# A two-level Winograd down-projection: the fourth right form gets its own room, the fifth product moves to the left buffer, three buffers are dealt anew and two weight sums are made earlier

## The chip, the cores and the metric

The kernel runs on one core of one Trainium2 chip. The metric is device time in microseconds of one execution. Work is split over TensorE (PE, with its weight loads shown as PEld), VectorE (DVE), ScalarE (ACT), GpSimd (POOL) and SyncE (SP). SP, ACT and POOL also issue DMA transfers, each on a queue of its own, and an engine works through its instructions in the order in which they were written.

## The reference, cut to what matters

2048 tokens of width 1024 go through two branches, which are mixed with a gate per token:

```python
g = sigmoid((x * gate_w).sum(-1, keepdims=True))
a = A_ref(x, wqkv, wo)          # 32 heads of 32; each token attends to 8 keys, 2 apart; then @ wo
b = B_ref(x, w_gate, w_up, w_down)   # h = gelu(x @ w_gate) * (x @ w_up), 3584 wide; then h @ w_down
return g * a + (1 - g) * b
```

Since both branches end in a matrix product, the kernel makes them one: the left side is `(1 - g) * h` beside `g * o` (o is the attention's output before `wo`), the right side `w_down` above `wo`. Everything that the change touches, but for two weight sums near the start, belongs to this last product, here called the down-projection.

## The kernel before, in words

**Memory.** Almost all of SBUF is one tile, `arena`, and the kernel deals out its addresses by hand. In the down-projection it holds ten buffers of 18 KB a partition, `bufs[0]` to `bufs[9]`, each 18 K-tiles by 512 columns in bf16. `plan` (L893) says for each half of the tokens (`s` = 0 and 1) which name lives in which buffer. All 8 PSUM banks are one tile, `banks`.

**Order of work.** The first 500 us are units of matmuls for the query, key, value, gate and up projections (L366), with a planner (`bg`, `due`, `run_bg`) that lays background tasks for DVE between them: each task has a priority and a unit from which it may run, and `due` finishes it before a given unit. `sums_qk` (L456) is such a task. Its two parts make the sums of the query and key weights that units 2 to 17 need, in eight DVE instructions (L463). From about 510 us on the order is written out by hand in `down(s)` (L1065), called for s = 0 and then for s = 1.

**The down-projection.** For each half of the tokens the left matrix is cut in four (`A11` to `A22`), the right in four (`R11` to `R22`), and Winograd's seven products take the place of eight. They need sums of the left quarters (`S`, `S2`, `AD`, on DVE at L925) and of the right quarters (`T1` to `T4`, made early and kept in HBM as `t_d`). Some of these seven products are made by plain matmuls (`mm`, L1074). The others go through `level2` (L1038), which applies Winograd's scheme once more: four in `down(0)` (on T1, T2, T3, T4 in this order) and six in `down(1)` (R11, T1, T2, T3, T4, R22), ten in all.

**One second-level product.** `forms_L` (L1000) makes four sums of quarters of the left operand in a buffer of their own, `forms_R` (L1008) four of the right operand. Of these four instructions the first, second and fourth fill three quarters of a right form buffer, and the third writes over a quarter of the right operand itself, `q(0, 1)`. Then `level2` runs seven products, each of two column blocks (j = 0, 1) of nine 128x256 matmuls (L1047):

```python
prod(0, 0, lq(0, 0), rq(0, 0), ...)   prod(0, 0, lq(0, 1), rq(1, 0))
prod(1, 0, lf[:, 0], rf[:, 0], lambda j: cp(p5d[:, j, :], c(1, 0, j)))
prod(1, 1, lf[:, 1], rf[:, 1], ...)   prod(1, 1, lf[:, 2], rq(0, 1), ...)
prod(0, 1, lf[:, 3], rq(1, 1))        prod(1, 0, lq(1, 1), rf[:, 2])
```

All accumulate in four banks, each used in two halves of 256 columns (`c(i, h, j)`). Between products ACT copies partial results from half to half (`cp`, L1052). The third product's state is kept aside in SBUF as fp32, two blocks of 128x256 (`part5`), and DVE adds it at the end (`join`, L1032). Before the change `part5` lies in the fourth quarter of the right form buffer, which no form uses.

**The forms are kept for the second half.** In `down(0)` `store_F` (L990) writes the forms of T1, T3 and T4 to HBM from ACT's queue in the middle of their `level2`: 576 KB for the form that lies in the T buffer, back into its quarter of `t_d` (L991), and 1728 KB for the three others, to `r_d` (L992). In `down(1)` SP loads T with `load_T` (L842) and the three forms with `load_F` (L988). SP issues its loads in the written order, and each load waits until its buffer has been read for the last time, and until the transfer that stood eight places ahead among those of SP and ACT has landed.

**Buffers that matter.** In `down(0)`: T1 and the right forms R6 share buffer 1, so `forms_R(R6)` may begin only when T1 has been read for the last time; T3 and S are in buffer 8; L5 and L7 in 4, R5 and R7 in 5; T4 in 9 and R4 in 7. In `down(1)` buffer 9 holds A21, buffer 1 R21 and buffer 7 A22, all loaded near the end of `down(0)`.

Of the kernel before, what the change touches and what calls it, by code (L numbers as in the profile page):

```python
# [9 lines left out]
ALU = mybir.AluOpType  # L10
# [58 lines left out]
def kernel(  # L69
# [55 lines left out]
    h_d = [[tc.dram_tile([P, 4, k, SC], BF16, name=f"h_d{s}{e}") for e, k in enumerate((NE_, NPAIR - NE_))] for s in range(2)]  # L125
    o_d = [[tc.dram_tile([P, NT, SC], BF16, name=f"o_d{s}{c}") for c in range(2)] for s in range(2)]
    t_d = [tc.dram_tile([P, NK, SC], BF16, name=f"t_d{k}") for k in range(4)]
    r_d = {k: tc.dram_tile([P, 3 * (NK // 2) * (SC // 2)], BF16, name=f"r_d{k}") for k in (1, 3, 4)}
    w_c = {k: tc.dram_tile([P, NK, SC], BF16, name=f"w_c{k[0]}{k[1]}") for k in ((0, 0), (1, 0), (1, 1))}
    z_d = tc.dram_tile([HK, S], F32, name="z_d")  # L130
    g_d = tc.dram_tile([2, S], BF16, name="g_d")
# [5 lines left out]
    with tc.manual_schedule(engines={mybir.EngineType.PE, mybir.EngineType.DVE, mybir.EngineType.Activation,  # L137
# [55 lines left out]
        def flat(a):  # L193
            return a.rearrange("p a b -> p (a b)")
# [261 lines left out]
        def sums_qk(part):  # L456
            L11, L12, L21, L22 = wq
            S1, S2, S4 = sq
            for o_, a, b_, op in (((S1, L21, L22, ALU.add), (S2, S1, L11, ALU.subtract)),
                                  ((L21, L11, L21, ALU.subtract), (S4, L12, S2, ALU.subtract)))[part]:  # L460
                for hk in range(0, HK, 2):
                    g = lambda t_: flat(t_[:, hk:hk + 2, :])
                    TT(out=g(o_), in0=g(a), in1=g(b_), op=op)  # L463
                    yield 1.14
# [21 lines left out]
        def at_end(n, fn):  # L486
            post.setdefault(n, []).append(fn)

        def due(n, t):
            at(n, t.finish)  # L490
# [296 lines left out]
            x_form3(1)  # L787
            yield 2.4

        due(Q0, bg(sums_qk(0), 1, 1))  # L790
        due(Q0 + 1, bg(sums_qk(1), 1, 2))
        due(Q0 + NT, bg(late_forms(), 3, Q0 + 1))
        bg(gate_task(0), 0, 0)
# [90 lines left out]
        def tf_close():  # L884
            while tf_q[0] < N1:
# [6 lines left out]

        plan = [dict(A11=4, R11=5, A12=2, R21=7, A21=6, A22=3, T1=1, T2=9, S=8, AD=0, L5=4, R5=5, L6=7, R6=1,  # L893
                     T3=8, L7=4, R7=5, T4=9, L4=1, R4=7, R22=6),
                dict(A11=0, R11=4, L1=5, R1=8, A12=3, A21=9, R21=1, A22=7, T1=2, AD=6, S=0, T2=8, L5=4, R5=5, L6=1, R6=2,
                     T3=0, L7=4, R7=5, T4=8, L4=2, R4=1, R22=9, L3=4, R3=5)]
        u2 = regf(R_U2, 4 * SC).rearrange("p (j n) -> p j n", j=4)
        qs = regf(R_QS, 4 * SC).rearrange("p (j n) -> p j n", j=4)
# [83 lines left out]
                    load_T(B[k], int(k[1]))  # L982

        KH, HN = NK // 2, SC // 2
        NF = 3 * KH * HN

        def load_F(rf, k):
            nc.sync.dma_start(out=flat(rf)[:, 0:NF], in_=r_d[k][:])  # L988

        def store_F(rf, b, k):  # L990
            nc.scalar.dma_start(out=t_d[k - 1][:, 0:KH, HN:SC], in_=quarter(b, 0, 1))  # L991
            nc.scalar.dma_start(out=r_d[k][:], in_=flat(rf)[:, 0:NF])  # L992

        def quarter(b, kh, h):
            return b[:, kh * KH:(kh + 1) * KH, h * HN:(h + 1) * HN]
# [12 lines left out]
        def forms_R(f, b):  # L1008
            f = quads(f)
            q = lambda kh, h: quarter(b, kh, h)  # L1010
            for o_, a, b_, op in ((f[:, 0], q(0, 1), q(0, 0), ALU.subtract), (f[:, 1], q(1, 1), f[:, 0], ALU.subtract),
                                  (q(0, 1), q(1, 1), q(0, 1), ALU.subtract), (f[:, 2], q(1, 0), f[:, 1], ALU.subtract)):
                TT(out=o_, in0=a, in1=b_, op=op)  # L1013
                yield 1.3

# [9 lines left out]
                nc.scalar.activation(out=two_banks(bk, i, 0), in_=omgrep[:, SUP:SUP + SC].rearrange("p (a b) -> p a b", a=2),  # L1025
                                     func=ACT.Copy, scale=0.0)

        def part5(rf):
            return flat(rf)[:, 3 * KH * HN:3 * KH * HN + 4 * HN].bitcast(F32).rearrange("p (j n) -> p j n", j=2)

        def join(bk, rf, i):
            TT(out=two_banks(bk, i, 1), in0=two_banks(bk, i, 1), in1=part5(rf), op=ALU.add)  # L1032

        def joins(bk, rf):
            for i in range(2):
                join(bk, rf, i)

        def level2(bk, L, R, lf, rf, mid=None, mid2=None):  # L1038
            p5d = part5(rf)
            lf, rf = quads(lf), quads(rf)  # L1040
            lq, rq = lambda r, c: quarter(L, c, r), lambda r, c: quarter(R, r, c)
            c = lambda i, h, j: banks[:, bk[2 * i + j], h * HN:(h + 1) * HN]

            def prod(i, h, l, r, then=None):
                for j in range(2):
                    for kt in range(KH):
                        nc.tensor.matmul(c(i, h, j), lhsT=l[:, kt, j * P:(j + 1) * P], rhs=r[:, kt, :], start=False,  # L1047
                                         stop=(kt == KH - 1), skip_group_check=True)
# [12 lines left out]
            if mid2:  # L1061
                mid2()
            prod(1, 0, lq(1, 1), rf[:, 2])

        def down(s):  # L1065
# [23 lines left out]
            if last:  # L1089
                run(scale_task(A12, s, 0, 0, NE_))  # L1090
                level2(XT, A11, B["R11"], B["L1"], B["R1"])
                rest = pieces(scale_task(A21, s, 1, 0, NE_), comb_task(AD, A11, A21, ALU.subtract))
                take(rest, 1)
                joins(XT, B["R1"])
                for j in range(4):
                    nc.scalar.copy(out=u2[:, j, :], in_=XP[j])
                run(rest)
                load_F(B["R5"], 1)
                loads(s, "T2")
            else:  # L1100
                for j in range(4):
                    mm(XP[j], A11, B["R11"], j, True, 0, NK - 2)
                    if j == 0:
                        yield
                for j in range(4):
                    mm(XP[j], A11, B["R11"], j, True, NK - 2, NK)
# [47 lines left out]
            level2(VT, AD, B["T3"], B["L7"], B["R7"],  # L1154
                   lambda: (zero_left(XT), last or store_F(B["R7"], B["T3"], 3)))
            fl, fr = forms_L(B["L4"], A22), forms_R(B["R4"], B["T4"])
            if last:
                fr = ()
# [8 lines left out]
            run(fr)  # L1167
            for j in range(4):
                if j % 2 == 0:
                    join(VT, B["R7"], j // 2)  # L1170
# [4 lines left out]
            level2(XT, A22, B["T4"], B["L4"], B["R4"],  # L1175
                   lambda: zero_left(VT) if last else store_F(B["R4"], B["T4"], 4))
            joins(XT, B["R4"])
            if not last:
                N = Bs(1)
                rest = pieces(scale_task(N["A11"], 1, 0, 0, NE_), woven(forms_L(N["L1"], N["A11"]), forms_R(N["R1"], N["R11"])))  # L1180
# [4 lines left out]
                loads(1, "A12", "A21", "R21", "A22")  # L1185
                zero_left(XT)
            if last:
                R3 = B["R3"]
                level2(VT, A12, B["R22"], B["L3"], R3, lambda: join(VT, R3, 1),
                       lambda: (join(VT, R3, 0), [add_out(VP[j], qs[:, j, :], 0, 1, j) for j in range(2)]))  # L1190
# [89 lines left out]
```

## Time and profile before

| | |
|---|---|
| time, median of 3 runs (lowest to highest) | 722.19 us (721.89 to 722.2) |
| the profiled execution: its time; its span | 722.87 us; 721.1 us |
| granted TensorE clock, mean | 1.000 |
| PE busy, of the span | 708.0 us, 98% |
| DVE busy | 672.9 us, 93% |
| ACT, POOL busy | 328.9 us (46%), 134.5 us (19%) |
| L1047, 1260 matmuls of 128x256 | 138.9 us busy |
| L1074, 282 matmuls of 128x512 in `down` | 62.7 us busy |
| `forms_L` L1005 (40) and `forms_R` L1013 (28), one instruction | 1354 and 1355 ns |
| ACT copy L1052 to SBUF, one | 373 ns |
| DMA busy share, 545.6 to 559.5 us; 602.1 to 647.5 us | 0.23; 1.02 to 1.03 |

The span runs from the first to the last instruction; the execution's time has 1.8 us more around it. A matmul's record is longer than its share of the engine (273 ns for one of 128x256, while 1260 of them keep PE busy for 138.9 us, so one follows the other after 0.11 us), because they are pipelined. Times within the span are counted from its start. In a timeline row the number in brackets is how long the engine had been idle and what ended that; "issue" there means that the profile names nothing.

### The profile page before, as it was taken

What the parts mean: (1) busy time and instruction counts of PE and PEld (TensorE: products, weight loads), DVE (VectorE), ACT (ScalarE), POOL (GpSimd) and SP (SyncE); (2) the same over time, 40 slices, a digit from 0 to 9 for tenths busy, and PEclk for the clock granted to TensorE, in tenths of its full rate; (3) what the DMA queues carried; (4) which work ended last, traced back from release to release, by engine and by line L of the source; (5) the groups of instructions that cost most, each with busy time, mean ns of one, the idle gap of its engine ahead of it and who ended that gap; (6) DMA issues with size and microseconds to landing.
All of it is one profiled execution on the core that took longest, in us unless ns stands there. A gap on an engine that the chain in (4) does not pass through costs nothing. (4 is left out here: it accounts for less than half of the span.)

```text
span 721.1 us, 10757 instructions
## 1 busy us (share of the span) xinstructions
PE 708.0 (98%) x4051; PEld 408.2 (57%) x4107; DVE 672.9 (93%) x721; ACT 328.9 (46%) x600; POOL 134.5 (19%) x233
## 2 busy tenths in 40 slices
PE   8999999999999999999999999999999999999997
PEld 4466656655544444444444444444447886748886
DVE  3699989999999999999998999999989999899997
ACT  4554446444457665555555555555322321132421
POOL 1333444133201331222210000000210002110011
PEclk9999999999999999999999999999999999999999
DMA  9976644279273758573943846371891899995941
GB/s 275 283 179 223 225 141 142 93 245 312 96 212 125 240 188 253 171 236 128 282 146 120 278 143 213 108 285 60 326 415 48 323 351 389 413 428 212 365 162 60
DMA packets 95252, 160.27 MB, mean 222 GB/s; under 512 B 19312, under 2 KB 71824, under 8 KB 90848
## 3 DMA queue, kind: packets, MB, share of 16 engines
q1 hardware_dynamic: 74992, 103.69, 42.1%
q0 software_dynamic: 15984, 48.29, 19.0%
q10 hardware_dynamic: 4224, 7.60, 3.0%
q8 instruction: 32, 0.52, 0.3%
q14 instruction: 20, 0.16, 0.1%
HBM read 110.40 MB, written 54.14 MB: 228 GB/s over the span
## 5 line engine op out<-in xcount | busy, mean ns | idle before, releaser
L366 PE MATMUL banks<-arena 128*128 128x512 bf16 x2136 | 472.5, 379 | 4.8 <-DVE arena L403 1.4
L366 PEld LDWEIGHTS <-arena 128*128 128x128 bf16 x2184 | 240.4, 111 | 236.4 <-issue 8.4
L1047 PE MATMUL banks<-arena 128*128 128x256 bf16 x1260 | 138.9, 273 | 1.3 <-DVE arena L1013 1.2
L1047 PEld LDWEIGHTS <-arena 128*128 128x128 bf16 x1260 | 123.0, 98 | 17.3 <-DVE arena L1013 1.5
L403 DVE TENSOR_TENSOR arena<-banks,arena 128x1024 bf16<-128x1024 f32 x78 | 95.2, 1221 | 12.4 <-PE banks L366 7.2
L389 ACT COPY arena<-banks 128x512 f32<-128x512 f32 x78 | 45.8, 587 | 130.7 <-PE banks L366 130.7
L374 ACT CAST arena<-banks 128x512 bf16<-128x512 f32 x102 | 59.8, 586 | 42.6 <-PE banks L366 42.3
L745 DVE TENSOR_TENSOR arena<-arena 128x2048 bf16<-128x2048 bf16 x64 | 77.0, 1220 | 0.5
L752 DVE TENSOR_TENSOR arena<-arena 128x2048 bf16<-128x2048 bf16 (+2 forms) x96 | 73.9, 776 | 1.0
L598 DVE TENSOR_TENSOR arena<-arena 128x2048 bf16<-128x2048 bf16 x64 | 74.7, 1219 | 0.1
L1074 PE MATMUL banks<-arena 128*128 128x512 bf16 x282 | 62.7, 379 | 0.7 <-DMA arena<-w_c 0.4
L260 POOL DMA_DIRECT2D h_d<-arena x28 | 20.4, 730 | 227.3 <-DVE arena L254 196.5
L396 ACT COPY banks<-banks 128x512 f32<-128x512 f32 x78 | 44.5, 570 | 22.5 <-PE banks L366 19.4
L1005 DVE TENSOR_TENSOR arena<-arena 128x2304 bf16<-128x2304 bf16 x40 | 53.3, 1354 | 0.5
L384 ACT COPY banks<-banks 128x512 f32<-128x512 f32 x78 | 45.0, 576 | 13.5 <-PE banks L366 12.1
L1052 ACT COPY banks<-banks 128x256 f32<-128x256 f32 x60 | 21.4, 356 | 61.5 <-PE banks L1047 61.3
L1074 PEld LDWEIGHTS <-arena 128*128 128x128 bf16 x288 | 28.1, 98 | 34.2 <-issue 0.7
L925 DVE TENSOR_TENSOR arena<-arena 128x2048 bf16<-128x2048 bf16 (+1 forms) x40 | 41.8, 1112 | 2.0 <-DMA arena<-h_d 2.0
L323 DVE TENSOR_TENSOR arena<-arena 128x1024 bf16<-128x1024 bf16 x60 | 38.7, 686 | 2.3 <-DMA arena<-in_B_w_up_dram 1.8
L1013 DVE TENSOR_TENSOR arena<-arena 128x2304 bf16<-128x2304 bf16 x28 | 37.8, 1355 | 2.0 <-issue 1.8
L372 ACT ACTIVATE arena<-banks 128x512 bf16<-128x512 f32 x54 | 32.3, 597 | 15.5 <-PE banks L366 15.5
L254 DVE TENSOR_TENSOR arena<-arena 128x2048 bf16<-128x2048 bf16 x28 | 34.1, 1216 | 1.9 <-ACT arena L251 1.4
(90 smaller groups left out, 436.1 us busy)
## 6 DMA issues: line engine op xcount, KB each, us to landing
arena<-t_d SPq DMA_DIRECT2D x8, 2304.0 KB, 15.8
h_d<-arena POOLq DMA_DIRECT2D x28, 512.0 KB, 4.3
arena<-w_c SPq DMA_DIRECT2D x12, 1152.0 KB, 13.1
t_d<-arena POOLq DMA_DIRECT2D x36, 256.0 KB, 4.4
arena<-h_d SPq DMA_DIRECT2D x6, 1536.0 KB, 9.1
arena<-in_B_w_gate_dram SPq DMA_DIRECT2D x15, 512.0 KB, 5.8
arena<-in_B_w_up_dram SPq DMA_DIRECT2D x15, 512.0 KB, 4.7
arena<-in_B_w_down_dram SPq DMA_DIRECT2D x28, 256.0 KB, 6.9
```

What stands on the lines that cost most here:

```text
L366: self.pe = nc.tensor.matmul(ps, lhsT=self.L[form](kt), rhs=rhs[:, kt, :], start=(start and kt == 0), stop=(kt == HK - 1), skip_group_chec ...
L374: nc.scalar.copy(out=o_, in_=i_)
L384: nc.scalar.copy(out=self.Y, in_=self.X)
L389: nc.scalar.copy(out=self.p5s, in_=self.V)
L396: nc.scalar.copy(out=self.Z, in_=self.Y)
L403: TT(out=self.T[:, :, c2s], in0=pair, in1=self.p5s.rearrange("p (o n) -> p o n", o=1).to_broadcast([P, 2, SC]), op=ALU.add)
L598: TT(out=dst, in0=q.rearrange("p (o s) -> p o s", o=1).to_broadcast([P, NWIN, AC]), in1=_win_ap(k, [[-DIL, NWIN], [1, AC]]), op=ALU.mult)
L745: TT(out=prod2[(t // 2) % 2][:, t % 2], in0=ab, in1=_win_ap(v[:, t, HALO:HALO + AC], [[SJ, NJ], [-DIL, NWIN], [1, SJ]]), op=ALU.mult)
L752: TT(out=out_, in0=h(0), in1=h(1), op=ALU.add)
L1005: TT(out=o_, in0=a, in1=b_, op=op)
L1047: nc.tensor.matmul(c(i, h, j), lhsT=l[:, kt, j * P:(j + 1) * P], rhs=r[:, kt, :], start=False, stop=(kt == KH - 1), skip_group_check=True)
L1074: nc.tensor.matmul(ps, lhsT=L[:, i, j * P:(j + 1) * P], rhs=R[:, i, :], start=(start and q == 0), stop=(q == NK - 1), skip_group_check=not ...
```

## The change

It has four parts.

1. `forms_R` writes its third instruction's result, the form from `q(1, 1) - q(0, 1)`, into the fourth quarter of the right form buffer and no longer over the T operand. `level2` reads it there. `store_F` becomes one transfer of the whole buffer (2304 KB) and no longer writes to `t_d`; `load_F` loads the whole buffer, and `r_d` grows to fit.
2. `part5` moves to the left form buffer, over the first left form. As that form is still read by the second column block, both `cp` calls now stand behind the whole product.
3. In `plan` for s = 1, R11 moves from buffer 4 to 8, L1 from 5 to 4 and R1 from 8 to 5. In `down(1)` the loads of R4 and R22 are written behind the joins of the preceding product, since R4's buffer now holds that product's `part5` (L6 is buffer 1 there).
4. The first two of the eight DVE instructions of `sums_qk` (the two halves of S1 = L21 + L22) are written at the end of unit 0.

```diff
-    r_d = {k: tc.dram_tile([P, 3 * (NK // 2) * (SC // 2)], BF16, name=f"r_d{k}") for k in (1, 3, 4)}
+    r_d = {k: tc.dram_tile([P, NK, SC], BF16, name=f"r_d{k}") for k in (1, 3, 4)}
...
-        due(Q0, bg(sums_qk(0), 1, 1))
+        sqk = bg(sums_qk(0), 1, 1)
+        due(Q0, sqk)
+        at_end(0, lambda: (sqk.step(), sqk.step()))
...
-                dict(A11=0, R11=4, L1=5, R1=8, A12=3, A21=9, R21=1, A22=7, T1=2, AD=6, S=0, T2=8, L5=4, R5=5, L6=1, R6=2,
+                dict(A11=0, R11=8, L1=4, R1=5, A12=3, A21=9, R21=1, A22=7, T1=2, AD=6, S=0, T2=8, L5=4, R5=5, L6=1, R6=2,
...
         def load_F(rf, k):
-            nc.sync.dma_start(out=flat(rf)[:, 0:NF], in_=r_d[k][:])
+            nc.sync.dma_start(out=rf, in_=r_d[k][:])
 
-        def store_F(rf, b, k):
-            nc.scalar.dma_start(out=t_d[k - 1][:, 0:KH, HN:SC], in_=quarter(b, 0, 1))
-            nc.scalar.dma_start(out=r_d[k][:], in_=flat(rf)[:, 0:NF])
+        def store_F(rf, k):
+            nc.scalar.dma_start(out=r_d[k][:], in_=rf)
...
             for o_, a, b_, op in ((f[:, 0], q(0, 1), q(0, 0), ALU.subtract), (f[:, 1], q(1, 1), f[:, 0], ALU.subtract),
-                                  (q(0, 1), q(1, 1), q(0, 1), ALU.subtract), (f[:, 2], q(1, 0), f[:, 1], ALU.subtract)):
+                                  (f[:, 3], q(1, 1), q(0, 1), ALU.subtract), (f[:, 2], q(1, 0), f[:, 1], ALU.subtract)):
...
-        def part5(rf):
-            return flat(rf)[:, 3 * KH * HN:3 * KH * HN + 4 * HN].bitcast(F32).rearrange("p (j n) -> p j n", j=2)
+        def part5(lf):
+            return flat(lf)[:, 0:4 * HN].bitcast(F32).rearrange("p (j n) -> p j n", j=2)
...
-            prod(1, 0, lf[:, 0], rf[:, 0], lambda j: cp(p5d[:, j, :], c(1, 0, j)))
+            prod(1, 0, lf[:, 0], rf[:, 0])
+            for j in range(2):
+                cp(p5d[:, j, :], c(1, 0, j))
             prod(1, 1, lf[:, 1], rf[:, 1], lambda j: cp(c(0, 1, j), c(1, 1, j)))
-            prod(1, 1, lf[:, 2], rq(0, 1), lambda j: cp(c(1, 0, j), c(1, 1, j)))
+            prod(1, 1, lf[:, 2], rf[:, 3], lambda j: cp(c(1, 0, j), c(1, 1, j)))
...
-            level2(VT, S, B["T1"], B["L5"], B["R5"], not last and (lambda: store_F(B["R5"], B["T1"], 1)))
+            level2(VT, S, B["T1"], B["L5"], B["R5"], not last and (lambda: store_F(B["R5"], 1)))
             run(forms_L(B["L6"], S2))
             rest = forms_R(B["R6"], B["T2"])
             take(rest, 2)
-            joins(VT, B["R5"])
+            joins(VT, B["L5"])
...
             if last:
                 load_F(B["R7"], 3)
                 loads(s, "T4")
-                load_F(B["R4"], 4)
-                loads(s, "R22")
                 rest = forms_L(B["L7"], AD)
                 take(rest, 2)
...
-            joins(XT, B["R6"])
+            joins(XT, B["L6"])
+            if last:
+                load_F(B["R4"], 4)
+                loads(s, "R22")
```

In the same way all other calls of `join` and `joins` take the left form buffer in place of the right one, and the other calls of `store_F` lose the T buffer. The built program has the same matmuls in the same order, and DVE the same instructions in the same order, but for the two sums, which now stand ahead of unit 0's L403. ACT issues three transfers fewer.

More of the change, by code (lines that the diff above doesn't have):

```diff
@@ L984 @@
         KH, HN = NK // 2, SC // 2
-        NF = 3 * KH * HN
         def load_F(rf, k):
-            nc.sync.dma_start(out=flat(rf)[:, 0:NF], in_=r_d[k][:])
-        def store_F(rf, b, k):
-            nc.scalar.dma_start(out=t_d[k - 1][:, 0:KH, HN:SC], in_=quarter(b, 0, 1))
-            nc.scalar.dma_start(out=r_d[k][:], in_=flat(rf)[:, 0:NF])
+            nc.sync.dma_start(out=rf, in_=r_d[k][:])
+        def store_F(rf, k):
+            nc.scalar.dma_start(out=r_d[k][:], in_=rf)
         def quarter(b, kh, h):
@@ L1026, in zero_left, with join, joins @@
                                      func=ACT.Copy, scale=0.0)
-        def part5(rf):
-            return flat(rf)[:, 3 * KH * HN:3 * KH * HN + 4 * HN].bitcast(F32).rearrange("p (j n) -> p j n", j=2)
-        def join(bk, rf, i):
-            TT(out=two_banks(bk, i, 1), in0=two_banks(bk, i, 1), in1=part5(rf), op=ALU.add)
-        def joins(bk, rf):
+        def part5(lf):
+            return flat(lf)[:, 0:4 * HN].bitcast(F32).rearrange("p (j n) -> p j n", j=2)
+        def join(bk, lf, i):
+            TT(out=two_banks(bk, i, 1), in0=two_banks(bk, i, 1), in1=part5(lf), op=ALU.add)
+        def joins(bk, lf):
             for i in range(2):
-                join(bk, rf, i)
+                join(bk, lf, i)
         def level2(bk, L, R, lf, rf, mid=None, mid2=None):
-            p5d = part5(rf)
+            p5d = part5(lf)
             lf, rf = quads(lf), quads(rf)
@@ L1093, in down @@
                 take(rest, 1)
-                joins(XT, B["R1"])
+                joins(XT, B["L1"])
                 for j in range(4):
@@ L1154, in down @@
             level2(VT, AD, B["T3"], B["L7"], B["R7"],
-                   lambda: (zero_left(XT), last or store_F(B["R7"], B["T3"], 3)))
+                   lambda: (zero_left(XT), last or store_F(B["R7"], 3)))
             fl, fr = forms_L(B["L4"], A22), forms_R(B["R4"], B["T4"])
@@ L1169, in down @@
                 if j % 2 == 0:
-                    join(VT, B["R7"], j // 2)
+                    join(VT, B["L7"], j // 2)
                 add_out(VP[j], qs[:, j, :], 1, 1, j)
@@ L1175, in down @@
             level2(XT, A22, B["T4"], B["L4"], B["R4"],
-                   lambda: zero_left(VT) if last else store_F(B["R4"], B["T4"], 4))
-            joins(XT, B["R4"])
+                   lambda: zero_left(VT) if last else store_F(B["R4"], 4))
+            joins(XT, B["L4"])
             if not last:
@@ L1187, in down @@
             if last:
-                R3 = B["R3"]
-                level2(VT, A12, B["R22"], B["L3"], R3, lambda: join(VT, R3, 1),
-                       lambda: (join(VT, R3, 0), [add_out(VP[j], qs[:, j, :], 0, 1, j) for j in range(2)]))
+                L3 = B["L3"]
+                level2(VT, A12, B["R22"], L3, B["R3"], lambda: join(VT, L3, 1),
+                       lambda: (join(VT, L3, 0), [add_out(VP[j], qs[:, j, :], 0, 1, j) for j in range(2)]))
                 for j in range(2, 4):
```

## The prediction

> **What bounds the kernel now.** I read the page's busy shares first, then the waits of PE, then the timeline around the longest waits of the down-projection, then the table by stage.
>
> ```profile
> PE 708.0 (98%) x4051; PEld 408.2 (57%) x4107; DVE 672.9 (93%) x721; ACT 328.9 (46%) x600; POOL 134.5 (19%) x233
> ...
> PE banks L366 <- DVE arena L403: 1.4, 4, 0.5
> PE banks L1047 <- DVE arena L1013: 1.2, 1, 1.2
> ...
> PE banks L366 <- DVE arena L463: 0.4, 1, 0.4
> PE banks L1074 <- DMA arena<-w_c: 0.4, 1, 0.4
> ```
>
> PE is busy 98% of the span, so only what shortens a wait of PE can gain, and every new wait of PE costs. The waits that the change touches are three: one for `forms_R`, one for a weight load and one for the weight sums. In the timeline the first looks so, at its source and at its end:
>
> ```profile
> 555.99 0.39 ACTq L991 DMA_DIRECT2D t_d<-arena  x1
> 556.50 0.55 ACTq L992 DMA_DIRECT2D r_d<-arena  x1
> 559.55 2.82 DVE L1013 TENSOR_TENSOR arena<-arena 128x2304 bf16<-128x2304 bf16 x2 [1.77 <-issue]
> 559.68 0.32 SPq L842 DMA_DIRECT2D arena<-t_d  x1
> ...
> 572.43 1.35 DVE L1013 TENSOR_TENSOR arena<-arena 128x2304 bf16<-128x2304 bf16 x1
> ...
> 581.09 1.36 DVE L1013 TENSOR_TENSOR arena<-arena 128x2304 bf16<-128x2304 bf16 x1
> 582.36 1.35 DVE L1005 TENSOR_TENSOR arena<-arena 128x2304 bf16<-128x2304 bf16 x1
> 582.50 1.53 PEld L1047 LDWEIGHTS <-arena 128*128 128x128 bf16 x15 [1.52 <-DVE arena L1013]
> 582.51 1.70 PE L1047 MATMUL banks<-arena 128*128 128x256 bf16 x14 [1.24 <-DVE arena L1013]
> ```
>
> DVE stood idle 1.77 us before `forms_R(R6)`. Its result goes into T1's buffer, and the store of T1's quarter (issued at 555.99, 3.5 us to landing, so 559.47) was still reading that. From 559.55 to 582 DVE has no other gap, and at the end of that chain PE waits for the third `forms_R` instruction of R7. PE's last matmul before it starts at 580.99, the next would follow 0.11 later and starts at 582.51: 1.41 us lost. Of `down(1)` two rows matter:
>
> ```profile
> 665.62 2.39 PEld L1047 LDWEIGHTS <-arena 128*128 128x128 bf16 x22 [0.21 <-issue]
> ...
> 683.48 2.52 PEld L1047 LDWEIGHTS <-arena 128*128 128x128 bf16 x24 [0.28 <-DVE arena L1005]
> ```
>
> Here too PE is just behind DVE's forms (R6 ends at 665.57, L7's third at 683.42). DVE runs without a real gap from 632.3 on, and starts there behind a join that waits for the end of the first product of `down(1)`. So in `down(1)` PE can't gain on DVE, and DVE follows PE's time at 631.
>
> ```profile
> core 0: us, PE busy (x) PEld busy (x) DVE busy (x) ACT busy (x) POOL busy (x), PEclk, DMA share, GB/s
> 573.20:588.40 15.20, 13.96 (x128) 12.27 (x127) 15.20 (x16) 3.92 (x10) 0.00 (x0) 1.00 0.88 353
> 617.60:631.40 13.80, 13.80 (x128) 12.28 (x126) 10.97 (x11) 3.79 (x10) 1.39 (x3) 1.00 1.02 411
> 631.40:647.50 16.10, 15.57 (x73) 7.07 (x73) 15.77 (x15) 4.03 (x8) 1.63 (x3) 1.00 1.02 428
> ```
>
> One such product is 13.7 us long; the third of `down(0)` is 15.2. The last two rows show that the DMA engines are full there (share 1.02).
>
> **The change part by part.** The sum is made against the profiled execution, 722.87 us (span 721.1 and 1.8 around it), which is 0.68 above the median.
>
> *The two sums ahead.* DVE is idle for 4.2 us before unit 0's L403 at 31.22. The later of the two weight loads lands at 28.79 (issued at 15.51, by the trace), two sums take 2.4 us (four take 4.62), so they end at 31.2, and L403 is not pushed. What is won, 2.4 us of DVE at 32 to 37, ends in another gap: L403 of unit 1 waits for PE until 37.26. The second part's four sums start behind it as before, at 38.5, and PE's wait for L463 at 42 to 43 (0.4 to 0.6) stays. Cost 0. Bounds: -0.6, if that wait went, which needs the order that the program doesn't have; and nothing the other way until the load is 1.3 us late, since the next to need L403's banks is ACT's copy at 33.74, and L403 ends at 32.45.
>
> *The fourth form out of place.* Same size; the 28 `forms_R` rows, in place or not, lie between 1349 and 1359 ns. 0, at most 0.01 us each.
>
> *The store's wait.* `forms_R(R6)` no longer waits for a store. DVE ends L6's forms at 557.78 and can go on at once: T2 landed at 541.4, and PE had done with the parts of T1 that are written over. The chain moves 1.77 ahead until `forms_R(R7)`, which would start at 570.66 in place of 572.43, and there T3 is late next. Its load waits for PE's end of the first product (issued at 559.68, not moved) and landed 11.9 us later, at 571.55. But by the trace's packets its first one starts at 563.6, just as the two stores drain. These take each DMA engine 72 packets of 512 B at 29 ns and 8 of 13,824 B at 0.52, 6.3 us; after, 8 of 18,432 B at the 0.69 of T3's own packets, 5.5 us. So T3 lands 0.8 sooner, at 570.8. DVE is then 1.6 ahead, R7's third instruction ends at 580.85, and PE needs it at 581.1. The wait goes whole: -1.41. Bounds: if T3 lands as before, DVE is 0.88 ahead and PE still loses 0.53: -0.88. More than -1.41 it can't be.
>
> *`part5` behind both blocks.* In each of the ten products the two copies stand behind the second block. The 256 fp32 of the first copy cover two of the nine K-tiles of the left form, so in the built program it waits for the second matmul of the second block only; the second copy waits for the ninth, as before. The next product's first matmul waits for the first copy, because both touch one bank. Count from the second block's start: second matmul at 0.11, copy 0.36 later (27 matmuls after the restart at 547.70 the copy row stands at 550.89), 0.37 long, so done at 0.84; PE restarts 0.05 after a copy (547.65 to 547.70) and is due at 0.98. Hidden, by 0.09 us. If that cover is gone, the other end is a copy that waits for the whole block: 0.36 + 0.37 + 0.05 - 0.11 = 0.67 a product, 6.7 for ten. I take 0.
>
> The Trainium skill (PSUM — Partial Sum Buffer, section on bank collisions) says that TensorE and another engine may not touch one bank in the same partitions at once, not even in different columns, and asks for guards by bank. That is why this wait can't be argued away by the different halves; no run here shows a collision. The sum is 0 by the rows above and up to +6.7 by the rule at its strictest.
>
> *Stores and loads of the forms.* A21's load no longer waits for the store of T4's quarter (issued at 616.75, where the transfer before it was issued at 602.67), R21's comes right behind. As the DMA engines are full from 602 to 650, the bytes land only about as much sooner as the stretch begins sooner (1.4) and packets get cheaper (0.7 for each store). PE's wait for R21 at 633.99 (0.58) goes, but DVE, moved by 1.4 only, holds PE at 665: 0, bound -0.58. Each form load grows by 576 KB, 1.4 us at 428 GB/s. R5 landed at 650.15 and is needed at 651.4, so it would land at 650.15 - 1.4 - 0.7 + 1.4 = 649.5 and be needed at 649.4 to 650.0: 0 to 0.1, which the wait at 665 swallows up to 0.8. T2, R7 and T4 have 3 us or more.
>
> *Buffers and order.* R11's new buffer (T3's) is free when A11's is, which stands ahead of it on SP. R1 needs r_d's second store landed (593.8), and starts at 612. R5's load now waits for 631.4 instead of 627.7, but queues behind T1 (landed 645.6). R4's load moves from 674.06 to the join's end (679.8 - 1.4), with R22 behind it: they land near 688 and 694, and are needed at 692 and 698. 0.
>
> Sum: 722.87 - 1.41 = 721.46 in this execution's time, 720.8 against the median.
>
> **The rivals.**
> - *T3 holds the chain.* It lands as before: -0.88, 721.3.
> - *PE keeps the R21 wait too.* It needs DVE 0.6 faster in `down(1)`; 722.19 - 1.99 = 720.2. Against it: the two rows at 665 and 683.
> - *R5 comes late.* If the DMA engines win nothing from the stores, R5 lands at 651.5, and PE, due at 649.4, loses 2.1; the wait at 665 returns 0.8. -1.41 + 1.3: 722.1, about no change.
> - *Slower: the `part5` copy.* Place: the first matmul of the fourth product, ten times. It decides against the change from 0.14 us each (1.41 / 10), that is a copy done 0.23 later than reckoned; at full price 722.19 - 1.41 + 6.7 = 727.5. For it: the cover is 0.09 us. Against: the built program's wait is for the second matmul.
>
> **How the numbers follow.** Likeliest case 0.56 (own range 720.4 to 721.1), T3 0.14, R21 0.10, R5 0.08, `part5` 0.12 (of which 0.02 cost under 1.41 in all). 0.2% is 1.44 us, about what a measurement of this kernel can tell from no change, and the likeliest case sits on that line: half of it (0.28) and R21 (0.10) give faster 0.38; its other half, T3, most of R5 and a little of `part5` give same 0.50; the rest, slower 0.12. The range reaches from 720.1 to 722.4 and leaves out the dear end of `part5`.
>
> **What would show it.** Right: `forms_R(R6)` without idle time before it, the `forms_R` wait gone from PE's list and the third product of `down(0)` 13.8 us long; one store on ACT's queue per product; first `part5` copies 0.22 us later than before, the second right behind, PE with no wait for ACT there; PE's wait for `w_c` gone and those at 665 and 683 (less 1.4) grown. Wrong: PE waiting for ACT L1051, idle time before `forms_R(R7)`, or PE waiting for r_d or T1.

## The result and the profile after

| | before | after |
|---|---|---|
| time, median of 21 runs each (lowest to highest) | 722.22 us (721.65 to 723.56) | 720.84 us (720.49 to 721.65) |
| ratio, with its 95% interval | | 0.998 (0.9973 to 0.9987) |
| the profiled execution: its time; its span | 722.87; 721.1 us | 720.80; 719.0 us |
| PE's time in the down-projection, see below | 206.67 us | 205.27 us |

The change gains 1.38 us (0.2%) in the medians, and the forecast of 720.8 came out. Single executions of one kernel differ by up to 2 us, and the profiled ones show where: in the loads of the first 17 us, and in before's trace a late load of the up weights, for which DVE waits 1.8 us at 383.68 and PE loses 1.0 behind it. So I also compare a stretch which these don't reach: from the start of the matmul ahead of PE's last wait for L403 (510.39 before, 509.54 after) to the end of PE's last matmul (717.06 and 714.81). It is 1.40 shorter. To turn a moment of after into before's time, add 0.85.

The page of the changed kernel, its engines and ACT's DMA queue (packets, MB, share):

```profile
PE 707.4 (98%) x4051; PEld 408.3 (57%) x4107; DVE 673.0 (94%) x721; ACT 328.5 (46%) x600; POOL 134.1 (19%) x233
...
q10 hardware_dynamic: 720, 7.60, 2.7%
```

PE's waits after (us in total, times, longest):

```profile
PE banks L366 <- DVE arena L403: 0.7, 2, 0.5
PE banks L1046 <- DVE arena L1012: 0.6, 1, 0.6
...
PE banks L366 <- DVE arena L463: 0.4, 1, 0.4
```

ACT's queue moves the same 7.60 MB in 720 packets that took 4224 before. The wait for `w_c` is gone from the list, the wait for the weight sums (L463) is as it was. One wait for `forms_R` (now L1012) is left, but at another place: the timeline of after, first the third product of `down(0)`, then `down(1)`.

```profile
554.82 27.34 PE L1046 MATMUL banks<-arena 128*128 128x256 bf16 x249
...
555.22 0.33 ACTq L991 DMA_DIRECT2D r_d<-arena  x1
556.49 2.81 DVE L1012 TENSOR_TENSOR arena<-arena 128x2304 bf16<-128x2304 bf16 x2
...
569.36 1.35 DVE L1012 TENSOR_TENSOR arena<-arena 128x2304 bf16<-128x2304 bf16 x1
...
577.77 0.37 ACT L1051 COPY arena<-banks 128x256 f32<-128x256 f32 x1 [2.85 <-PE banks L1046]
578.02 1.35 DVE L1012 TENSOR_TENSOR arena<-arena 128x2304 bf16<-128x2304 bf16 x1
578.54 0.37 ACT L1051 COPY arena<-banks 128x256 f32<-128x256 f32 x1 [0.40 <-PE banks L1046]
...
659.74 3.00 PE L1046 MATMUL banks<-arena 128*128 128x256 bf16 x26
661.96 2.81 DVE L1012 TENSOR_TENSOR arena<-arena 128x2304 bf16<-128x2304 bf16 x2
663.36 19.89 PE L1046 MATMUL banks<-arena 128*128 128x256 bf16 x179 [0.62 <-DVE arena L1012]
...
681.22 1.86 PEld L1046 LDWEIGHTS <-arena 128*128 128x128 bf16 x18 [0.28 <-DVE arena L1004]
```

`forms_R(R6)` at 556.49 has no idle time before it (1.77 before), PE runs 249 matmuls from 554.82 on without a gap, and the third `forms_R` instruction of R7 (578.02) is done well ahead of PE. The first `part5` copy stands at 577.77 and the second right behind its block, with PE undisturbed. In `down(1)` PE now waits 0.79 for R6's form where it lost 0.20. The table by stage, the third product of `down(0)` and the start of `down(1)`:

```profile
core 0: us, PE busy (x) PEld busy (x) DVE busy (x) ACT busy (x) POOL busy (x), PEclk, DMA share, GB/s
572.35:586.15 13.80, 13.80 (x129) 12.36 (x127) 13.80 (x15) 3.92 (x10) 0.00 (x0) 1.00 0.96 403
...
629.20:645.00 15.80, 15.69 (x75) 7.26 (x75) 15.53 (x15) 4.02 (x9) 1.62 (x3) 1.00 1.02 430
```

The time that PE lost in the stretch, by place (the step from one matmul's start to the next, less the usual step of that form), closes the account, for this pair and for all runs below. The stretch differs from before's by what the lost times differ, to within 0.1 (the two runs with a moved `part5` also lose at the copy):

| kernel | third product, 581 | weight loads, 630 to 633 | R5, 649 | R6's form, 662 to 665 | L7's form, 681 to 683 | stretch |
|---|---|---|---|---|---|---|
| before | 1.41 | 0.58 | | 0.20 | 0.16 | 206.67 |
| after | | | | 0.79 | 0.17 | 205.27 |
| sums undone | | | | 0.78 | 0.16 | 205.24 |
| before + sums | 1.40 | 0.69 | | | 0.16 | 206.65 |
| after + T1's store | 1.83 | | | 0.78 | 0.16 | 207.09 |
| before - T1's store | | 1.33 + 0.75 | | | | 206.36 |
| before - T1's and T4's stores | | | | 0.78 | 0.16 | 205.25 |
| after + T4's store | | 0.32 | 0.75 | | | 205.34 |
| before + `part5`, plan | 1.45 | 0.74 | | | 0.16 | 206.73 |
| after, `part5` at K-tile 2 | | | | 0.67 | | 206.15 |
| after, `part5` at K-tile 5 | | | | 0.34 | | 209.09 |
| after, forms woven | | | | | 0.57 | 204.87 |
| and L7's form earlier | | | | | | 204.28 |
| and second sums earlier | | | | | | 204.29 |

(An empty field is under 0.15 us.)

### The profile page after: what moved, and what is told of

The parts are those of the page before. It is cut to its first block, busy times and chain, and to the rows that moved or that the text cites. A ratio compares the mean times of both kernels' runs of the same rounds, so it can differ in the third digit from the quotient of the medians.

```text
span 719.0 us, 10748 instructions
## 1 busy us (share of the span) xinstructions
PE 707.4 (98%) x4051; PEld 408.3 (57%) x4107; DVE 673.0 (94%) x721; ACT 328.5 (46%) x600; POOL 134.1 (19%) x233
## 5 line engine op out<-in xcount | busy, mean ns | idle before, releaser
L403 DVE TENSOR_TENSOR arena<-banks,arena 128x1024 bf16<-128x1024 f32 x78 | 95.2, 1221 | 11.0 <-PE banks L366 5.4
L1004 DVE TENSOR_TENSOR arena<-arena 128x2304 bf16<-128x2304 bf16 x40 | 53.3, 1352 | 0.5
L1012 DVE TENSOR_TENSOR arena<-arena 128x2304 bf16<-128x2304 bf16 x28 | 37.7, 1352 | 0.2
```

The costliest lines, as they stand in the source:

```text
L403: TT(out=self.T[:, :, c2s], in0=pair, in1=self.p5s.rearrange("p (o n) -> p o n", o=1).to_broadcast([P, 2, SC]), op=ALU.add)
```

## The experiments

The theory was that of the prediction: the removed wait of `forms_R(R6)` for T1's store is the whole gain, everything else costs and brings nothing. The rivals gave a part of it to the sums, to the lighter DMA work or to the moved buffers.

**The sums.** Once undone in the changed kernel, once alone in the kernel before.

```diff
-        sqk = bg(sums_qk(0), 1, 1)
-        due(Q0, sqk)
-        at_end(0, lambda: (sqk.step(), sqk.step()))
+        due(Q0, bg(sums_qk(0), 1, 1))
```

> The changed kernel with the two weight sums back at their old place. Theory (the removed wait for the store is the whole gain, the sums are worth nothing): 720.8 us, within 0.2 of the changed kernel, with PE's wait for L463 near 42.6 at 0.4 to 0.7 as in both. Rival (the sums ahead of unit 1 carry a part of the gain): slower than the changed kernel by up to 1.4, so 721.4 to 722.2.

Measured: 720.68 us (720.43 to 721.17), ratio to before 0.9979 (0.997 to 0.9988), as the changed kernel.

The same three lines the other way round, in the kernel before:

> The kernel before with the two weight sums forward and nothing else. Theory: 722.2 us, no change, because DVE's second idle stretch (the wait of L403 of unit 1 for PE) still ends at the same moment and the other four sums start behind it. Rival: the wait for L463 near 42 goes, 0.4 to 0.6 faster, 721.6 to 721.8.

Measured: 722.44 us (721.68 to 723.74), ratio 1.0006 (0.9997 to 1.0015). PE loses 0.59 at L463 in both runs, as in before and after. The two sums carry nothing. In the changed kernel they run behind their load at 29.19 and push the sums that follow forward, and DVE's wait for PE ahead of unit 1's L403 grows from 0.28 to 2.55 us.

**T1's store put back into the changed kernel**, on ACT's queue ahead of the `r_d` store:

```diff
-            level2(VT, S, B["T1"], B["L5"], B["R5"], not last and (lambda: store_F(B["R5"], 1)))
+            level2(VT, S, B["T1"], B["L5"], B["R5"], not last and (lambda: (nc.scalar.dma_start(
+                out=t_d[0][:, 0:KH, HN:SC], in_=quarter(B["T1"], 0, 1)), store_F(B["R5"], 1))))
```

> The changed kernel with one store added: T1's quarter (512-byte packets, 576 KB) is stored once more on ACT's queue ahead of the r_d store of the first product, so that forms_R(R6), which writes over T1's buffer, has to wait for its landing again. Theory: DVE idles about 1.8 us before forms_R(R6) and, as T3 then lands behind 7.6 us of stores, PE waits 1.4 to 1.8 in the third product again: 722.2 to 722.6 us. Rival (the gain came from less DMA work in down(1) or from other parts of the change): it stays at 720.8 to 721.2.

Measured: 722.61 us (722.18 to 722.91), ratio to before 1.0002 (0.9993 to 1.0011): the whole gain is gone. The timeline of this kernel:

```profile
555.49 0.39 ACTq L1126 DMA_DIRECT2D t_d<-arena  x1
556.05 0.50 ACTq L991 DMA_DIRECT2D r_d<-arena  x1
559.05 2.82 DVE L1012 TENSOR_TENSOR arena<-arena 128x2304 bf16<-128x2304 bf16 x2 [1.89 <-issue]
...
572.36 1.36 DVE L1012 TENSOR_TENSOR arena<-arena 128x2304 bf16<-128x2304 bf16 x1 [0.34 <-DMA arena<-t_d]
...
581.03 1.35 DVE L1012 TENSOR_TENSOR arena<-arena 128x2304 bf16<-128x2304 bf16 x1
582.44 0.83 PE L1046 MATMUL banks<-arena 128*128 128x256 bf16 x6 [1.67 <-DVE arena L1012]
```

The idle time of DVE is back (1.89), T3 now also comes 0.34 late for R7's first form, and PE loses 1.83 in the third product. So the store alone brings back the wait, and with it the loss. Whether taking the store away is enough, the next run asks.

**T1's store alone taken out of the kernel before.**

```diff
-            nc.scalar.dma_start(out=t_d[k - 1][:, 0:KH, HN:SC], in_=quarter(b, 0, 1))
+            if k > 1:
+                nc.scalar.dma_start(out=t_d[k - 1][:, 0:KH, HN:SC], in_=quarter(b, 0, 1))
```

> The kernel before without the one store of T1's quarter in down(0); with it the product of down(1) that loads T1 again finds the plain quarter in the place of the fourth form, so that part of the output is another. Nothing else is changed. Theory: the idle 1.77 us before forms_R(R6) goes and PE's 1.41 in the third product with it: 720.8 us (720.7 to 721.3). Rival (other parts of the change carry the gain): 722.2, as before.

Measured: 721.51 us (720.6 to 722.71), ratio 0.999 (0.9982 to 0.9999): a part of the gain only, in the median. The profiled execution is the slowest of the eleven; 1.0 us of it is the late load of the up weights, as in before's trace. In its timeline DVE and PE run through at 557 to 583, as the theory says, but PE stops twice later:

```profile
553.80 29.42 PE L1048 MATMUL banks<-arena 128*128 128x256 bf16 x268
...
557.98 2.81 DVE L1014 TENSOR_TENSOR arena<-arena 128x2304 bf16<-128x2304 bf16 x2
...
597.28 0.38 ACTq L992 DMA_DIRECT2D t_d<-arena  x1
...
616.52 1.45 SPq L815 DMA_DIRECT2D arena<-h_d  x2
...
631.48 2.10 PE L1075 MATMUL banks<-arena 128*128 128x512 bf16 x9 [1.17 <-DMA arena<-w_c]
...
634.16 1.02 PE L1075 MATMUL banks<-arena 128*128 128x512 bf16 x4 [0.58 <-DMA arena<-w_c]
```

In before's timeline the same store, the same load and the one wait stand at:

```profile
598.59 0.38 ACTq L991 DMA_DIRECT2D t_d<-arena  x1
...
616.75 1.27 SPq L815 DMA_DIRECT2D arena<-h_d  x2
...
633.99 13.76 PE L1074 MATMUL banks<-arena 128*128 128x512 bf16 x62 [0.42 <-DMA arena<-w_c]
```

The first wait is for the weights of the first plain product of `down(1)`, the second for R21. Both loads stand on SP's queue behind A21's (616.52), which waits for T4's store, issued at 597.28. The stretch starts 0.10 later here than in before, which the differences that follow allow for. T4's store goes out 1.4 us sooner than in before, but lands only 0.3 sooner (616.44, in before 616.68). R21's load waits for one landing more, that of the `r_d` store eight places ahead (622.08; R21's load goes out at 622.14). The two loads land at 631.34 and 634.12, in before at 631.16 and 633.94: although PE is 1.4 ahead, no sooner. The table by stage shows what the DMA engines do meanwhile. Four stretches of this kernel (of before, the DMA shares are 0.56, 0.94, 0.99 and 0.80):

```profile
core 0: us, PE busy (x) PEld busy (x) DVE busy (x) ACT busy (x) POOL busy (x), PEclk, DMA share, GB/s
566.00:572.00 6.00, 6.00 (x57) 5.39 (x56) 6.00 (x6) 3.51 (x10) 0.00 (x0) 1.00 0.16 67
572.00:578.00 6.00, 6.00 (x57) 5.37 (x56) 6.00 (x9) 1.72 (x4) 0.00 (x0) 1.00 0.94 347
578.00:584.00 6.00, 6.00 (x57) 5.39 (x56) 6.00 (x6) 2.40 (x7) 0.00 (x0) 1.00 0.98 416
584.00:590.00 6.00, 6.00 (x57) 5.37 (x56) 6.00 (x6) 1.53 (x4) 0.00 (x0) 1.00 0.92 306
```

The DMA engines are nearly full from 572 on, when PE's end of the second product lets the next loads go (issued at 571.57 here, at 571.47 in before). That lies ahead of the place where PE gains. From there to 650 the same bytes have to pass, and PE, coming 1.4 us earlier, only waits for them.

That is one execution. The three fastest of the eleven took 720.60 to 720.63 us, 1.0 to 1.1 less than before's fastest of the same measurement (721.67), where the stretch of the trace accounts for 0.3. They weren't profiled; most of the gain seems to have come through in them.

**T1's and T4's stores both taken out of the kernel before**, T3's left in:

```diff
-            nc.scalar.dma_start(out=t_d[k - 1][:, 0:KH, HN:SC], in_=quarter(b, 0, 1))
+            if k == 3:
+                nc.scalar.dma_start(out=t_d[k - 1][:, 0:KH, HN:SC], in_=quarter(b, 0, 1))
```

> The kernel before without the stores of T1's and of T4's quarter in down(0) (T3's stays); the two products of down(1) that load T1 and T4 again find plain quarters in the place of the fourth forms, so that part of the output is another. The run without T1's store alone won back the third product, but PE then waited 1.3 and 0.7 us for the two weight loads at 630 and 633, which stand on the SP queue behind T4's store. Theory (the changed kernel's gain needs both stores gone, the one to win 1.4 and the other to let it through): A21's load is issued near 602 in place of 616.5, no wait for the weight loads, 0.8 us of PE's wait back at 662 for R6's form, 720.8 us (720.5 to 721.2). Rival (the rest of the change, buffers and later loads, is needed too): 721.5 as without T1's store alone.

Measured: 721.35 us (720.5 to 722.09), ratio 0.9982 (0.9973 to 0.9991). In PE's list of waits no line is left for `w_c`, and the wait for `forms_R` (here L1014) is that of the changed kernel:

```profile
PE banks L1048 <- DVE arena L1014: 0.6, 1, 0.6
```

A21's load goes out at 601.25, R21 lands at 630.12, and the losses of the stretch (0.78 and 0.16) and its length (205.25) are those of the changed kernel. Its lowest run is also that of the changed kernel; its runs scatter more. With the two stores gone the down-projection of before has the changed kernel's time in the trace; new buffers and moved loads aren't needed for it. (It also writes 1152 KB and loads 1728 KB less than the changed kernel.) By the times alone this kernel and the one without T1's store can't be told apart: their intervals overlap, and each has three runs of eleven at 720.63 or less. That T4's store makes the difference rests on the two traces.

**T4's store put back into the changed kernel.**

```diff
-                   lambda: zero_left(VT) if last else store_F(B["R4"], 4))
+                   lambda: zero_left(VT) if last else (nc.scalar.dma_start(out=t_d[3][:, 0:KH, HN:SC],
+                       in_=quarter(B["T4"], 0, 1)), store_F(B["R4"], 4)))
```

> The changed kernel with T4's quarter stored once more (512-byte packets, 576 KB) ahead of the r_d store of the fifth product, so that A21's load, which goes into T4's buffer, waits for its landing again. Theory: A21's load is issued near 615 in place of 601.7, PE waits 1.3 and 0.7 for the weight loads at 630 and 633, and its wait of 0.8 at 662 goes, so that some 1.1 of the changed kernel's gain is given back: 721.9 us (721.3 to 722.3), with the third product of down(0) still at 13.8 us. Rival (the weight loads have time to spare): 720.8.

Measured: 720.79 us (720.55 to 722.4), ratio 0.9981 (0.9972 to 0.999): the expectation failed, the time is that of the changed kernel. The timeline:

```profile
596.31 0.38 ACTq L1178 DMA_DIRECT2D t_d<-arena  x1
...
613.62 1.19 SPq L817 DMA_DIRECT2D arena<-h_d  x2
...
631.46 13.76 PE L1075 MATMUL banks<-arena 128*128 128x512 bf16 x63 [0.15 <-DMA arena<-w_c]
...
649.88 2.34 PE L1046 MATMUL banks<-arena 128*128 128x256 bf16 x20 [0.58 <-DMA arena<-r_d]
```

A21's load does wait for the store, but goes out at 613.62, and the weights of the first product are in time: T3's quarter store is gone too, and the DMA engines are ahead by then: the two weight loads issued near 589 and 590 land at 602.1 and 605.8 (in before's time), 2.4 sooner than in the kernel without T1's store alone. PE loses 0.32 for R21 and 0.75 for R5, 1.07 together, and in return the 0.96 that it lost for R6's and L7's forms. What the loads cost and what DVE costs in `down(1)` take each other's place. The larger of the two counts, not their sum. In these traces T4's store costs only where the loads are as late as in before.

**`part5`.** Alone in the kernel before, with the plan and the moved loads (the core of it; forms and stores stay as they were):

```diff
-            return flat(rf)[:, 3 * KH * HN:3 * KH * HN + 4 * HN].bitcast(F32)...
+            return flat(lf)[:, 0:4 * HN].bitcast(F32)...
...
-            prod(1, 0, lf[:, 0], rf[:, 0], lambda j: cp(p5d[:, j, :], c(1, 0, j)))
+            prod(1, 0, lf[:, 0], rf[:, 0])
+            for j in range(2):
+                cp(p5d[:, j, :], c(1, 0, j))
```

> The kernel before with only part5 moved over the left form's first two K-tiles, both copies behind both blocks, the buffers dealt by the changed plan and R4's and R22's loads moved behind the join; the fourth form stays in place, the stores stay as before, the sums stay. Theory (the copies are hidden, by 0.09 us by the rows, and the wait for T1's store stays): 722.2 us, 721.9 to 722.6, no wait of PE for ACT's copy line and forms_R(R6) with its 1.8 us of idle time before it. Rival (the guard of the bank bites): from 0.5 slower up to 6.7 slower, 722.7 to 728.9.

Measured: 722.53 us (721.78 to 723.41), ratio 1.0 (0.9991 to 1.0009). PE waits nowhere for the copies, and the stretch is before's to 0.06. To see whether the copies are hidden by much or by little, `part5` was moved on in the left form, so that its first half lies over K-tiles that PE reads later:

```diff
-            return flat(lf)[:, 0:4 * HN].bitcast(F32)...
+            return flat(lf)[:, 2 * HN:6 * HN].bitcast(F32)...
```

> The changed kernel with part5 two K-tiles further on in the left form (K-tiles 2 to 5 in place of 0 to 3 of half a form's row), so that the first copy waits for the fourth matmul of the second block instead of the second. Theory (by the working of the prediction the first copy is done at 0.33 + 0.36 + 0.37 = 1.06 us after the block's start, PE restarts 0.05 later and is due at 0.98): 0.13 lost in each of ten products, some 0.3 of it taken back where PE waits for VectorE anyway, so about +1.0, 721.8 us (721.4 to 722.2). Rival (the copy's cover is larger than 0.09 or PE needs no guard there): 720.8, no change from the changed kernel.

Measured: 721.78 us (721.43 to 723.04), ratio 0.9993 (0.9984 to 1.0002); the stretch is 0.88 longer than the changed kernel's. PE loses 0.12 at the first matmul of the fourth product in each of the ten products (0.13 expected), and 0.29 less at R6's and L7's forms.

With `5 * HN:9 * HN` in the same line:

> The changed kernel with part5 five K-tiles further on in the left form, so that the first copy waits for the seventh matmul of the second block. Theory: copy done at 0.66 + 0.36 + 0.37 = 1.39, PE back at 1.44 against 0.98 due: 0.46 lost in each of ten products, about 0.6 of the 4.6 taken back at PE's other waits: 724.8 us (723.8 to 725.4), with PE waiting for ACT's copy line ten times. Rival (no guard, or a cover larger than reckoned by 0.46): 720.8.

Measured: 724.55 us (724.37 to 726.25), ratio 1.0034 (1.0022 to 1.0047). Its list of waits:

```profile
PE banks L1046 <- ACT arena L1051: 2.9, 10, 0.3
...
PE banks L1046 <- DVE arena L1012: 0.2, 1, 0.2
```

and one of the ten places in its timeline:

```profile
550.56 0.65 ACT L1051 COPY arena<-banks 128x256 f32<-128x256 f32 x2 [3.55 <-PE banks L1046]
550.99 2.23 PE L1046 MATMUL banks<-arena 128*128 128x256 bf16 x19 [0.29 <-ACT arena L1051]
```

PE restarts 0.43 after the first copy starts (its length of 0.37 and 0.05) and loses 0.45 each time (0.46 expected), ten times 4.5, of which 0.62 come back at R6's and L7's forms: 3.88 by that sum, 3.82 by the stretch. Both runs together confirm the cover of the prediction, a little under 0.1 us: two matmuls later the copy costs 0.12, five later 0.45, and as the change has it, nothing. The Trainium skill (PSUM — Partial Sum Buffer, section on bank collisions) asks for a guard between two engines on one bank even where they touch different columns; the trace agrees that PE is held here, 0.45 us each, by a copy from the other half of the bank.

**What binds after the change.** PE's two losses in `down(1)` are for DVE's forms. First L6's and R6's forms woven, joins after four of the eight:

```diff
-            run(forms_L(B["L6"], S2))
-            rest = forms_R(B["R6"], B["T2"])
-            take(rest, 2)
+            if last:
+                rest = woven(forms_L(B["L6"], S2), forms_R(B["R6"], B["T2"]))
+                take(rest, 4)
+            else:
+                run(forms_L(B["L6"], S2))
+                rest = forms_R(B["R6"], B["T2"])
+                take(rest, 2)
```

> The changed kernel with, in the last down-projection only, the forms of L6 and R6 issued alternately (left, right, left, right) ahead of the two joins, in place of three left forms, two right forms, joins. Theory: PE's wait of 0.79 at 662 for R6's form goes, but VectorE, which has no free time there, then holds PE at 681 for L7's third form by about as much more: 720.8 us, at best 0.2 faster. Rival (the waits at 662 and 681 are independent): 0.6 to 0.8 faster, 720.0 to 720.2.

Measured: 720.32 us (720.04 to 721.39), ratio to before 0.9973 (0.9964 to 0.9983). Between the two: the 0.79 went, and 0.41 of it came back at 681 (the last number in the brackets of the timeline is PE's idle time; by starts it lost 0.57, 0.17 in the changed kernel):

```profile
679.91 5.28 DVE L1004 TENSOR_TENSOR arena<-arena 128x2304 bf16<-128x2304 bf16 x4
...
681.32 3.88 PE L1046 MATMUL banks<-arena 128*128 128x256 bf16 x34 [0.41 <-ACT banks L1051]
```

The list names ACT, but PE starts 0.06 after the first of DVE's four forms ends (679.91 + 1.35). Then L7's third form ahead of DVE's adds as well:

```diff
                 rest = forms_L(B["L7"], AD)
-                take(rest, 2)
+                take(rest, 3)
```

> The run with the woven forms, and with L7's third left form taken ahead of the adds that were before it, so that PE finds it ready at 681 too. Theory: both waits of PE go (0.79 and 0.17 in the changed kernel) and nothing later takes them, as VectorE's later work in that part ends before PE needs it: 719.9 us (719.7 to 720.3). Rival (the wait moves on to a later form or to the output adds): 720.6 to 720.8.

Measured: 719.85 us (719.43 to 719.96), ratio 0.9963 (0.9951 to 0.9976). PE has no gap from 659.78 to 685 any more:

```profile
659.78 25.49 PE L1046 MATMUL banks<-arena 128*128 128x256 bf16 x232
```

And the second part's first two sums at the end of unit 1:

```diff
-        due(Q0 + 1, bg(sums_qk(1), 1, 2))
+        sq1 = bg(sums_qk(1), 1, 2)
+        due(Q0 + 1, sq1)
+        at_end(1, lambda: (sq1.step(), sq1.step()))
```

> The run before it, with the first two of the second part's sums (L21' = L11 - L21) issued at the end of unit 1, ahead of that unit's own chain, the way the changed kernel does with the first part's. Theory: PE's wait of 0.6 for L463 near 42.6 goes: 719.3 us (719.1 to 719.8). Rival (another wait in the same stage takes its place, as it did when the first part's sums went forward): 719.9.

Measured: 719.26 us (718.91 to 719.54), ratio 0.9954 (0.9941 to 0.9968). PE's wait for L463 is gone from its list and nothing stands in its place. This is the fastest version of the study, 1.6 us below the changed kernel by the medians, which is what the lost times say (0.96 in `down(1)` and 0.59 at L463).

## Why the prediction was right, and where it was not

**The number was right:** 720.84 for 720.8, and by the account above for the reasons it gives: -1.41 in the third product, -0.58 at the weight loads, +0.59 back at R6's form, as "DVE, moved by 1.4 only, holds PE at 665" says. The split behind it was wrong, as far as one trace shows it. Of the signs that it names, the wait at 683 did not grow (0.16 before, 0.17 after).

- *The two sums ahead*, 0: right (shown with and without them). The wait for L463 stays at 0.59.
- *The fourth form out of place*, 0: its row reads 1352 ns on the mean (1348 to 1359) after the change.
- *The store's wait*, -1.41: right for the change as a whole. T3 was mis-sized: it landed 9.6 us after its issue, 2.2 sooner than before, not 0.8, so the lower bound of -0.88 was too cautious. The third form of R7 ended at 579.37, 580.22 in before's time, for 580.85 forecast. By the packets, 15 of the 16 DMA engines did end T3's load 0.8 sooner (568.05, that is 568.90 in before's time, for 569.68). In before the last engine ended another 0.8 later, at 570.46, and the landing came 1.1 behind it; after the change it came 0.4 behind. A last engine 0.8 to 0.9 behind shows in all four kernels that store T1's quarter in 512-byte packets, and in none of the ten others (0.3 at most). Why it falls behind is not known.
- *`part5`*, 0: right, and narrowly, as reckoned. The first copy came 0.21 later than before's, for 0.22 forecast. The cover of 0.09 was real: the two kernels with a later copy cost 0.88 and 3.82 where 1.0 and 4.0 were worked out.
- *Stores and loads*, 0: right as a total (-0.58 and +0.59), but one step of it failed. "The bytes land only about as much sooner as the stretch begins sooner (1.4)" lets the loads follow PE by themselves. In the trace without T1's store they didn't. The DMA engines were nearly full from about 572, with loads that PE's second product releases, ahead of the gain, and A21's load and those behind it waited for T4's store. The loads landed no sooner than before, and PE lost at them most of what it had won: 206.36, against 205.25 without T4's store as well. So the step was not worth 0 but some 1.1 of the 1.4 us in these two traces, and the 1.41 of the step before it only about 0.3 by itself. By the medians it was worth 0.5, and in the three fastest runs, which weren't profiled, about 1. In the changed kernel R21 landed 2.9 sooner (in before's time) and R5 at 649.0 instead of the forecast 649.5. The loads behind T4's store had gone out 14 us earlier (A21's at 601.74, 602.6 in before's time, in place of 616.75). For R21 that is enough: without T1's and T4's stores, but with T3's left in, it landed 3.3 sooner.
- *Buffers and order*, 0: right. R4 and R22 landed at 687.6 and 693.1 in before's time, for 688 and 694.

Of the rivals, T3 did not hold the chain. PE did not keep R21's wait; what it would have taken is shown by the two runs that rearrange DVE's forms. R5 came late only with T4's store put back, by 0.75, and then it took the place of DVE's waits. The dear `part5` copy needed two K-tiles more.

One thing stays open: the runs of the kernels without the larger `r_d` stores scatter more (the run without T1's and T4's stores from 720.5 to 722.09, with the same stretch in the trace), and three of the five such kernels that were profiled, before among them, show the late load of the up weights, none of the other nine. Whether that is chance or belongs to the change wasn't settled. It would count toward the medians, not the stretch.

## What to carry to other kernels

- A wait that goes is worth only what the next resource lets through. Ask not only which instruction is late next on the same engine, but when the transfers that follow are released. If they are released ahead of the gain and the DMA engines are full behind it, they can land at the same moment, and the gain is waited away.
- Terms of a sum may be right together and wrong apart: in the traces removing one store won 0.3 us, both 1.4, and putting one back cost next to nothing. One trace is one execution: the fastest runs without the one store were 1.0 faster than before's. Where two waits lie in one chain, price the larger of them, not each by itself.
- A copy hidden by 0.09 us can be trusted if its start is counted from single rows; moving it by two or five matmuls shows how far it may go.

## What was not expected of the hardware

The same store of 576 KB in 512-byte packets, in before, from the answers on DMA issues in two windows (555 to 563 and 598 to 618 us; KB, us from issue to landing):

```profile
t_d<-arena ACTq DMA_DIRECT2D x1, 576.0 KB, 3.5
...
t_d<-arena ACTq DMA_DIRECT2D x1, 576.0 KB, 18.1
```

It took 3.5 us where it had the DMA engines to itself, and 18.1 where SP's loads in packets of 9,216 and 12,288 bytes ran beside it. By the packets of the second case only 25 to 39 a microsecond of the 512-byte ones passed from 602 to 609, on all engines, where some 550 a microsecond passed in the first. In these 7 us 237 of them passed beside 225 of SP's large ones, about one for one. So it was with the same store in two other traces (247 beside 226 without T1's store, 246 beside 226 with T4's store put back). Here the store's time beside large packets went by the number of its packets and not by its bytes, and whoever waited for its landing (A21's load, and all of SP's queue behind it) was late with it.
